# Two fused expert layers behind attention: the order of weight conversions, row loads and stores changed

## The chip, the core and the metric

One core of one Trainium2 chip runs the whole program. The metric is the time of one execution in microseconds (us). TensorE (PE) multiplies, VectorE (DVE), ScalarE (ACT) and GpSimd (POOL) do the rest, and DMAs move data between the chip's memory and the core. SyncE (SP) does no arithmetic: it issues DMAs, in the order of the program, and where one of them has to wait, all behind it on SP stand. GpSimd can issue DMAs too, on a queue of its own.

## The reference

```python
q_s = exp(q - max(q, -1)); q_s /= sum(q_s, -1) + 1e-09      # (8, 8, 576, 64)
k_s = exp(k - max(k, 2));  k_s /= sum(k_s, 2) + 1e-09
kv = einsum('bhsd,bhse->bhde', k_s, v)
x = einsum('bhsd,bhde->bhse', q_s, kv)                       # as rows: (4608, 512)
g = x @ w_gate                                               # 512 x 1536
x = (g * sigmoid(g) * (x @ w_val)) @ w_out                   # 1536 x 512
h = x @ w_in                                                 # 512 x 2048
y = where(h > 0, h, exp(min(h, 0)) - 1) @ w_out2             # 2048 x 512
```

All of it is float32.

## The kernel before

**Tiling.** The 4608 rows are nine blocks of 512. The first expert layer has d_ff 1536, twelve tiles f of 128; the second 2048, sixteen tiles. A float32 product is made of three products: each operand is split into a rounded part (hi, by ACT) and the rest (lo, by DVE).

**Phase A** (`run_a`, to about 570 us) takes the first six f of all nine blocks. A block i has 6 x 3 places (f, s): at s = 0 the gate projection, at s = 1 the value projection (`proj`, L828 to L832), at s = 2 the product with w_out of the f before (L809 to L811). The table `PLAN` puts the attention of block i+1 between them. At (2,1) and (2,2) the second half of the queries is normalized (L524 to L527, DVE) and turned, at (2,2) SP issues the loads of the turned queries (`in0`, tile qT, from dq), and at (4,0) they are multiplied with kv on PE (L639), into the PSUM banks "t" and "c".

The weights that later stages need arrive as raw blocks of 512 KB and are converted beside phase A, one stage of the pipe per call of `conv()`: SP loads a block (raw), ACT scales it (L199, tile cg), DVE makes its bits with three instructions (L214, L217 into PSUM bank "c", L221 out of it into the tile cd). There is one bank "c", so the queries' product into "c" waits until L221 has read it. In blocks 2 to 7 `conv()` is called at s = 2 of all six f and at (3,0): seven times. Rows of x of the block before are summed by GpSimd (L659, two per call of `store_x`) and stored to xs at (1,0) and (1,2).

Block 8 has `side_last` in place of the attention: it loads the rows of the first pair of blocks (`v_load`, eight DMAs of 256 KB), sums them on GpSimd (`v_sums`, eight subtractions L1389) and splits the results for the next phase (`x_make`, L1422 on ACT, L1423 on DVE).

**Phase B** (`run_b`, about 570 to 1000 us) does the other six f for pairs of blocks (0,1), (2,3), (4,5), (6,7), then for block 8 alone. A 2 x 2 block product takes seven products, M1 to M7 (L1118). A unit has six steps; the stationary rows s come two steps ahead into a ring of two, loaded by SP (`load_sb`, from sfg/sfv the first time, then from sbg/sbv). Between the steps the unit loads the next pair's rows (`v_load`), sums them (`v_sums`), and rebuilds the outputs of finished pairs for phase 2: SP loads yr from ys, GpSimd subtracts (L1019, tile xt), ACT and DVE split (L1063, L1035), GpSimd stores xd. The unit's end makes the split rows of the next pair. A block's rows are closed by DVE (L1474, tile ev) and stored to ys.

**Phase 2** (`run_2`, `step`) is the second layer in two halves over the same units, again with seven products per step, each summed by DVE (`add`, L1242) from PSUM into tiles u, the first copied there by ACT (L1264). The stationary rows of the next f are split inside a step: `split_pop()` does the ACT half (L1074), `lo_pop()` the DVE half (L1077). After half 0 of a unit its rows are stored to y2 (L1209).

The engines do their instructions in the order of this code; no scheduler reorders them.

Of the kernel before, what the change touches and what calls it, by code (L numbers as in the profile page):

```python
# [17 lines left out]
def kernel(  # L18
# [1068 lines left out]
    def split_pop():  # L1087
        if split_now:
            split_now.pop(0)()
            return True  # L1090
# [110 lines left out]
    def evac(half, blk, js):  # L1201
        if half == 0:
            ev = ev_p.tile([128, KD, TB], FP32, tag="ev", name="ev")
            for j in js:
                if j % 2:
                    nc.scalar.activation(out=ev[:, j, :], in_=acc["2", blk][j], func=ACTF.Copy)
                else:
                    nc.vector.tensor_copy(ev[:, j, :], acc["2", blk][j])
            nc.sync.dma_start(out=y2[blk], in_=ev)  # L1209
            return  # L1210
        ev = y2_t[blk]
        dst = out[blk * TB:(blk + 1) * TB, :]
        if blk >= TURN:
            dst = dst.rearrange("(j p) n -> p j n", j=4)
        else:
            dst = dst.rearrange("(p j) n -> p j n", j=4)
        for j in js:
            nc.vector.tensor_tensor(ev[:, j, :], acc["2", blk][j], ev[:, j, :], op=ALU.add)
            if len(js) == 1:
                nc.sync.dma_start(out=dst[:, j], in_=ev[:, j])  # L1220
        if len(js) > 1:
            nc.sync.dma_start(out=dst, in_=ev)
# [21 lines left out]
    def step(u, gs_, mid, after=None):  # L1244
        lo_pop()
        splits_due()
        d11, d12, d21, d22 = (dst_of(u, gs_, rc) for rc in ((0, 0), (0, 1), (1, 0), (1, 1)))
        prev = tail.pop() if tail else None
        p0 = p_bank(0)
        product(p0, "M1", u, gs_, True)  # L1250
        if prev:
            s0, b12, b21, e12, e21 = prev
            w = cg()
            add(w, s0, b12)
            add(s0, s0, b21)
        p1 = p_bank(1)
        product(p1, "M6", u, gs_, True)
        if prev:
            k21 = elu_act(s0, False)
        split_pop()  # L1260
        p3 = p_bank(3)
        product(p3, "M7", u, gs_, True)
        s1 = cg()
        nc.scalar.activation(out=s1, in_=p0, func=ACTF.Copy)  # L1264
        if prev:
            elu_stt(k21)
            elu_max(k21)
            k12 = elu_act(w, True)
        add(s1, s1, p1)
        if prev:  # L1270
            elu_hi(k21, e21)
        lo_pop()
        split_pop()
        split_pop()
        u3 = cg()
        add(u3, s1, p3)
        p2 = p_bank(2)
        product(p2, "M5", u, gs_, True)
        product(p0, "M2", u, gs_, False)
        add(u3, u3, p2)  # L1280
        if prev:
            elu_lo(k21, e21)
            elu_stt(k12)
            elu_max(k12)
        lo_pop()
        while split_pop():
            pass
        if after is None:
            k22 = elu_act(u3, False)
            if prev:  # L1290
                elu_hi(k12, e12)
            lo_pop()
            ends = [m() for m in mid]
            product(p2, "M3", u, gs_, False)
            product(p3, "M4", u, gs_, False)
            k11 = elu_act(p0, True)
            elu_stt(k22)
            elu_max(k22)
            if prev:
                elu_lo(k12, e12)  # L1300
            elu_hi(k22, d22)
            elu_stt(k11)
            elu_max(k11)
            elu_hi(k11, d11)
            elu_lo(k22, d22)
            elu_lo(k11, d11)
            for e in ends:
                if e:
                    e()
            tail.append((s1, p2, p3, d12, d21))  # L1310
            rot()
            return
        product(p2, "M3", u, gs_, False)
        product(p3, "M4", u, gs_, False)
        if prev:
            k11 = elu_act(p0, False)
            elu_hi(k12, e12)
            elu_lo(k12, e12)
        lo_pop()
        w = cg()  # L1320
        add(w, s1, p2)
        add(s1, s1, p3)
        for m in mid:
            m()
        if not prev:
            k11 = elu_act(p0, False)
        k21 = elu_act(s1, True)
        elu_stt(k11)
        elu_max(k11)
        elu_hi(k11, d11)  # L1330
        k22 = elu_act(u3, False)
        elu_stt(k21)
        elu_max(k21)
        elu_lo(k11, d11)
        elu_hi(k21, d21)
        elu_lo(k21, d21)
        elu_stt(k22)
        elu_max(k22)
        elu_hi(k22, d22)
        elu_lo(k22, d22)  # L1340

        def rest():
            k12 = elu_act(w, True)
            elu_stt(k12)
            elu_max(k12)
            elu_hi(k12, d12)
            elu_lo(k12, d12)

        rot()
        after(rest)  # L1350
# [17 lines left out]
    V = {}  # L1368
    V_SRC = {"M1": 0, "M7": 1, "M2": 2, "M3": 3, "M5": 4, "M6": 5, "M4": 6}

    def v_load(u):
        w = TB if len(u) == 2 else TB // 2
        V[u] = []
        for c in range(2):
            t, t_ = (
                w2_pool[0].tile([128, 4 - part, TB], FP32, tag=f"s{2 + c}{part}", name="v")
                for part in range(2)
# [93 lines left out]
    def b_evac(blk):  # L1471
        ev = yp_t.pop(blk)
        for c in range(KD):
            nc.vector.tensor_tensor(ev[:, c, :], acc["b", blk][c], ev[:, c, :], op=ALU.add)  # L1474
        nc.sync.dma_start(out=ys[blk], in_=ev)

    T, n_T = {}, [0]

# [192 lines left out]
    def unit_b(n, u, nxt, carry):  # L1671
        a, b = u
        for k, (kind, g) in enumerate(B_STEPS):
# [19 lines left out]
            ahead = B_STEPS[(k + 2) % len(B_STEPS)], n == 0 and k < len(B_STEPS) - 2  # L1693
            step_b(u, kind, g, mid, tick, ahead, last)
            load_sb(ahead[0], (1,), first=ahead[1])
            if k == 0:
                v_load(nxt)
            if k == 2:
                v_sums(nxt)
        b_D(a, F1 - 2)  # L1700
        ev = b_D(a, F1 - 1)
# [10 lines left out]
        if single:  # L1712
            x_make(nxt, head[2:])
            rest = ("M2", "M3", "M4")
        else:
            rest = ("M7", "M5", "M2")
        for op in rest:
            x_alloc(nxt, (op,))
            x_make(nxt, (op,))
# [5 lines left out]
    def single_b(u, carry):  # L1725
        NG1 = HALF // 2
        nxt = units[0]
        for g in range(NG1):
# [23 lines left out]
            if g == 0:  # L1752
# [2 lines left out]
                X[nxt] = ({}, [])  # L1755
                x_big(nxt, X_HEAD)
            if g == 1:
                load_s(0)
                load_s(1, 1)
                x_small(nxt, X_MID[2:], ANY)  # L1760
        while xd_st["k"] < 6 or later:
            aged()
            lo_pop()
# [21 lines left out]

    def side_last(ff, s):
        u = units[0]
        if (ff, s) == (0, 2):
            v_load(u)
        if (ff, s) == (1, 2):  # L1790
            v_sums(u)
            load_sb(B_STEPS[0], first=True)
            load_sb(B_STEPS[1], first=True)
        if (ff, s) == (2, 2):
# [2 lines left out]
            split_pop()  # L1797
        if (ff, s) == (2, 0):
            x_alloc(u, ("M1", "M6"))
            for op in ("M7", "M5", "M2"):  # L1800
                todo.append(lambda op=op: (x_alloc(u, (op,), ("w",)), x_make(u, (op,))))
            for f in range(HALF, F1):
                todo.append(lambda f=f: load_ob(f, ("w",)))
# [99 lines left out]
                st[name]()  # L1903

    pend_b = []

    def run_a():
        for i in range(NB):
# [5 lines left out]
            for f in range(HALF):  # L1914
                for s in range(3):
# [20 lines left out]
                    if i == 1 and (stage["split"] < NA1 or s == 2):  # L1936
                        conv()
                    side_1a(i, f, s)
                    if i and f == 1 and s != 1:
                        store_x(i - 1, s // 2)  # L1940
                    if s == 1:
                        silu_val(t, val, ("a", i, f))
                    elif s == 2:
                        split_lo()
                    if 2 <= i < NB - 1 and (s == 2 or (f, s) == (3, 0)):
                        conv()
                    if i == NB - 1:
                        if s:
# [122 lines left out]
```

## Time and profile before

| | before |
|---|---|
| runs | 1758.6, 1758.87, 1762.76 us; median 1758.87 |
| the profiled execution | 1761.39 us |
| its span | 1759.7 us |
| PE busy | 1682.6 us (96%), 8228 matmuls |
| DVE, ACT, POOL busy | 1200.3, 806.6, 309.6 us |
| mean granted TensorE clock | 0.984 |

The span runs from the first to the last instruction of the profiled execution, and 1.7 us lie around it. Waits are idle times of an engine, put down to what ended them. A row of the timeline is one instruction or a run of like ones: start, length, engine, line, operation, out<-in, shapes, and in brackets the idle time before it with what ended that. The granted clock of a window is its mean over that window; TensorE runs at 2.4 GHz (1.00) or at 1.2 GHz (0.5).

### The profile page before, as it was taken

The numbers are of one execution on the slowest core, as the hardware profiler recorded it, in microseconds if no ns is written. First come the engines' busy times: TensorE is split into PE (matmuls) and PEld (weight loads), VectorE is DVE, ScalarE is ACT, GpSimd is POOL, SyncE is SP. The second block draws the span as 40 slices with busy tenths as digits, with TensorE's granted clock in tenths as the row PEclk, the third lists the DMA queues.
The fourth block names the chain that finished last, engine by engine and source line by source line (L and its number), as shares of the span: only waits on it lengthen the run. The fifth ranks groups of instructions, "written<-read, shape, count | busy, mean of one in ns | idle before, by whom it ended". The sixth has DMA issues, their size and how long they took to land.

```text
span 1759.7 us, 22267 instructions
## 1 busy us (share of the span) xinstructions
PE 1682.6 (96%) x8228; PEld 1374.9 (78%) x8228; DVE 1200.3 (68%) x1808; ACT 806.6 (46%) x1347; POOL 309.6 (18%) x346
## 2 busy tenths in 40 slices
PE   5899989999998899999999989999999999999999
PEld 4677777777877688787888868888888988888887
DVE  7867898878756574665666686757674866556474
ACT  4644244334334332332424474646564655445362
POOL 3613342344215202232231000000000000000000
PEclk9999999999999999999999999999999999999999
DMA  9467977796574667577686927262623434251511
GB/s 284 115 159 204 280 216 213 232 288 214 191 248 176 227 242 243 216 286 303 249 321 224 390 67 269 96 248 77 250 84 126 165 153 164 99 196 68 215 48 72
DMA packets 183532, 348.29 MB, mean 198 GB/s; under 512 B 49920, under 2 KB 121856, under 8 KB 169984
## 3 DMA queue, kind: packets, MB, share of 16 engines
q1 hardware_dynamic: 167712, 285.79, 49.1%
q0 software_dynamic: 15712, 61.09, 9.0%
q8 instruction: 64, 1.05, 0.2%
q14 instruction: 44, 0.36, 0.1%
HBM read 230.69 MB, written 116.14 MB: 197 GB/s over the span
## 4 chain that ended last, share of the span: by engine, by line
PE 65%; DVE 16%; DMA 8%; ACT 4%; issue 3%; POOL 2%; SPq 1%; DVEq 0%; POOLq 0%; ACTq 0%
PE p L1118 26%; PE y L811 10%; PE y L809 10%; PE y L810 10%; PE a L828 3%; PE a L829 3%; PE a L832 3%; DMA s<-sd 2%; DVE u L1242 1%; DMA s<-sfv 1%; DVE g L847 1%; DVE c L217 1%; DMA s<-sbv 1%; POOL v L1389 1%; DVE c L214 1%
## 5 line engine op out<-in xcount | busy, mean ns | idle before, releaser
L1242 DVE TENSOR_TENSOR u<-u,p 128x512 f32<-128x512 f32 x315 | 216.0, 686 | 218.5 <-PE p L1118 200.0
L1118 PE MATMUL p<-xp,s 128*128 128x512 f32 x1344 | 323.2, 394 | 20.3 <-DVE u L1242 19.7
L1118 PEld LDWEIGHTS p<-xp,s 128*128 128x128 f32 x1344 | 253.5, 190 | 78.3 <-DVE u L1242 24.8
L1118 PE MATMUL p<-xs,s 128*128 128x512 f32 (+1 forms) x1260 | 272.6, 370 | 3.4 <-ACT u L1264 1.8
L1118 PEld LDWEIGHTS p<-xs,s 128*128 128x128 f32 x1260 | 222.5, 190 | 44.8 <-ACT u L1264 2.4
L811 PE MATMUL y<-w,g 128*128 128x512 f32 x576 | 225.1, 391 | 0.6
L810 PE MATMUL y<-w,g 128*128 128x512 f32 x576 | 224.3, 389 | 0.7 <-DVE w L1077 0.7
L809 PE MATMUL y<-w,g 128*128 128x512 f32 x576 | 224.2, 389 | 0.0
L828 PE MATMUL a<-x,w 128*128 128x512 f32 x424 | 173.3, 409 | 6.4 <-DVE th L859 5.1
L829 PE MATMUL a<-x,w 128*128 128x512 f32 x424 | 170.0, 401 | 0.0
L1137 DVE SCALAR_TENSOR_TENSOR th<-e,th 128x512 f32<-128x512 f32 x144 | 99.3, 690 | 101.0 <-ACT e L1132 99.6
L1130 ACT ACTIVATE e<-u 128x512 f32<-128x512 f32 x108 | 67.7, 627 | 150.9 <-DVE u L1242 150.9
L811 PEld LDWEIGHTS y<-w,g 128*128 128x128 f32 x576 | 108.1, 188 | 26.2 <-DVE g L1166 3.9
L810 PEld LDWEIGHTS y<-w,g 128*128 128x128 f32 x576 | 108.2, 188 | 23.3 <-DVE w L1077 1.1
L809 PEld LDWEIGHTS y<-w,g 128*128 128x128 f32 x576 | 108.1, 188 | 22.3
L1157 ACT ACTIVATE g<-th 128x512 fp32r<-128x512 f32 (+1 forms) x160 | 91.3, 580 | 67.9 <-DVE th L1143 67.9
L1166 DVE TENSOR_TENSOR g<-th,g 128x512 fp32r<-128x512 f32 (+1 forms) x160 | 100.0, 635 | 32.0 <-ACT g L1157 29.7
L832 PE MATMUL a<-x,w 128*128 128x512 f32 x424 | 115.0, 393 | 0.6 <-POOL w L254 0.6
L828 PEld LDWEIGHTS a<-x,w 128*128 128x128 f32 x424 | 82.4, 194 | 29.9 <-DVE th L859 5.5
L841 ACT ACTIVATE g<-th 128x512 fp32r<-128x512 f32 x54 | 34.0, 629 | 153.7 <-DVE th L859 153.7
L829 PEld LDWEIGHTS a<-x,w 128*128 128x128 f32 x424 | 82.8, 195 | 16.8
L832 PEld LDWEIGHTS a<-x,w 128*128 128x128 f32 x424 | 81.0, 191 | 18.4 <-POOL w L254 1.0
(222 smaller groups left out, 2803.0 us busy)
## 6 DMA issues: line engine op xcount, KB each, us to landing
xp<-xd SPq DMA_DIRECT2D x32, 1024.0 KB, 10.2
xs<-xd SPq DMA_DIRECT2D x51, 512.0 KB, 7.0
xd<-xst POOLq DMA_DIRECT2D x42, 512.0 KB, 9.0
raw<-in_moe_w_out SPq DMA_DIRECT2D x26, 512.0 KB, 5.6
s<-sbg SPq DMA_DIRECT2D x10, 1024.0 KB, 7.0
s<-sbv SPq DMA_DIRECT2D x10, 1024.0 KB, 6.9
yp<-ev SPq DMA_DIRECT2D x9, 1024.0 KB, 3.9
xs<-ev POOLq DMA_DIRECT2D x18, 512.0 KB, 4.1
```

The costliest lines, as they stand in the source:

```text
L809: nc.tensor.matmul(out=ps, lhsT=wh, rhs=xh, start=first, stop=False)
L810: nc.tensor.matmul(out=ps, lhsT=wh, rhs=xl, start=False, stop=False)
L811: nc.tensor.matmul(out=ps, lhsT=wl, rhs=xh, start=False, stop=last)
L828: nc.tensor.matmul(out=ps, lhsT=wh, rhs=x[:, c, 0, :], start=(c == 0), stop=False)
L829: nc.tensor.matmul(out=ps, lhsT=wh, rhs=x[:, c, 1, :], start=False, stop=False)
L832: nc.tensor.matmul(out=ps, lhsT=wl, rhs=x[:, c, 0, :], start=False, stop=(c == KD - 1))
L1118: nc.tensor.matmul(out=out_, lhsT=w, rhs=x, start=first and (q, c, k) == (0, 0, 0), stop=(c, k) == (1, 2), skip_group_check=True,)
L1130: nc.scalar.activation(out=e, in_=h, func=ACTF.Relu, scale=-1.0)
L1137: nc.vector.scalar_tensor_tensor(out=t, in0=e, scalar=1.0, in1=t, op0=ALU.add, op1=ALU.mult)
L1157: nc.scalar.activation(out=gt[:, 0, at:at + n], in_=t[:, q * n:(q + 1) * n], func=ACTF.Copy)
L1166: nc.vector.tensor_tensor(gt[:, 1, at:at + n], t[:, q * n:(q + 1) * n], gt[:, 0, at:at + n].bitcast(FP32), op=ALU.subtract,)
L1242: nc.vector.tensor_tensor(o, a, b, op=ALU.add)
```

## The change

In phase A the seven calls of `conv()` in blocks 2 to 7 stand in a table: the one at (3,2) is moved to (2,0). `store_x` is called at (2,1) and (3,0), in place of (1,0) and (1,2). In block 8 the two halves of `v_load` come at (0,0) and (0,1) in place of (0,2), and `v_sums` at (1,1) in place of (1,2). In phase B a half of `v_load` comes after step 1 and the other after step 2, in place of all of it after step 0, and `v_sums` after step 3 in place of step 2; the last rows of a pair are split in the order M2, M5, M7. The ys and y2 rows are stored by GpSimd's queue. In phase 2 one early `split_pop()` and one `lo_pop()` go, and the sum u3 comes ahead of the two splits that are left. In the unit of block 8 a split is put ahead of two loads.

```diff
-            nc.sync.dma_start(out=y2[blk], in_=ev)
+            nc.gpsimd.dma_start(out=y2[blk], in_=ev)
...
         product(p1, "M6", u, gs_, True)
         if prev:
             k21 = elu_act(s0, False)
-        split_pop()
         p3 = p_bank(3)
         product(p3, "M7", u, gs_, True)
         s1 = cg()
...
             elu_hi(k21, e21)
-        lo_pop()
+        u3 = cg()
+        add(u3, s1, p3)
         split_pop()
         split_pop()
-        u3 = cg()
-        add(u3, s1, p3)
         p2 = p_bank(2)
...
-    def v_load(u):
+    def v_load(u, cs=(0, 1)):
         w = TB if len(u) == 2 else TB // 2
-        V[u] = []
-        for c in range(2):
+        V.setdefault(u, [])
+        for c in cs:
...
-        nc.sync.dma_start(out=ys[blk], in_=ev)
+        nc.gpsimd.dma_start(out=ys[blk], in_=ev)
...
-            if k == 0:
-                v_load(nxt)
-            if k == 2:
+            if k in (1, 2):
+                v_load(nxt, (k - 1,))
+            if k == 3:
                 v_sums(nxt)
...
-            rest = ("M7", "M5", "M2")
+            rest = ("M2", "M5", "M7")
...
             if g == 1:
+                x_small(nxt, X_MID[2:], ANY)
                 load_s(0)
                 load_s(1, 1)
-                x_small(nxt, X_MID[2:], ANY)
...
-        if (ff, s) == (0, 2):
-            v_load(u)
+        if (ff, s) in ((0, 0), (0, 1)):
+            v_load(u, (s,))
+        if (ff, s) == (1, 1):
+            v_sums(u)
         if (ff, s) == (1, 2):
-            v_sums(u)
...
-            for op in ("M7", "M5", "M2"):
+            for op in ("M2", "M5", "M7"):
...
+    CONV_AT = ((0, 2), (1, 2), (2, 0), (2, 2), (3, 0), (4, 2), (5, 2))
...
-                    if i and f == 1 and s != 1:
-                        store_x(i - 1, s // 2)
+                    if i and (f, s) in ((2, 1), (3, 0)):
+                        store_x(i - 1, f - 2)
...
-                    if 2 <= i < NB - 1 and (s == 2 or (f, s) == (3, 0)):
+                    if 2 <= i < NB - 1 and (f, s) in CONV_AT:
                         conv()
```

On DVE, in a query block (here block 3), this is what the moved conversion passes: bd is the scaled kv, qr and q the queries' sums and the normalized queries, th and g the activation of the first layer and its lo half, km the keys' maximum, x the rows of the next block out of the banks "t" and "c".

```order
 L493 TENSOR_TENSOR bd_172<-t,rs 128x256
+L214 TENSOR_SCALAR c<-cg 128x512
+L217 SCALAR_TENSOR_TENSOR c<-cg,c 128x512
+L221 SCALAR_TENSOR_TENSOR cd<-raw,c 128x512
 L524 TENSOR_SCALAR qr<-qr 128x16
 L525 RECIPROCAL qr<-qr 128x16
```

```order
 L396 TENSOR_TENSOR km<-km,kr 64x512
 L847 TENSOR_TENSOR g<-th,g 128x512
-L214 TENSOR_SCALAR c<-cg 128x512
-L217 SCALAR_TENSOR_TENSOR c<-cg,c 128x512
-L221 SCALAR_TENSOR_TENSOR cd<-raw,c 128x512
 L648 TENSOR_TENSOR x<-t,x 128x512
 L648 TENSOR_TENSOR x<-c,x 128x512
```

The three instructions stood last ahead of the instructions L648 that read the queries' products, and stand now ahead of the second normalization, before the activation's product at (2,1).

SP in the first unit of phase B, before: s are stationary rows (sfg, sfv where they come from), v the next pair's rows out of xs, yp the partial outputs of block 8.

```order
L1440 DMA s_5055<-sfg_128 128x4x256
L1440 DMA s_5097<-sfg_129 128x3x256
L1386 DMA v<-xs_176 128x512
L1386 DMA v<-xs_177 128x512
L1386 DMA v<-xs_176 128x512
L1386 DMA v<-xs_177 128x512
L1386 DMA v<-xs_176 128x512
L1386 DMA v<-xs_177 128x512
L1386 DMA v<-xs_176 128x512
L1386 DMA v<-xs_177 128x512
L885 DMA yp_191<-ev 128x2048
L1440 DMA s_5162<-sfv_134 128x4x256
```

The same place now:

```order
L1438 DMA s_5055<-sfg_128 128x4x256
L1438 DMA s_5097<-sfg_129 128x3x256
L885 DMA yp_191<-ev 128x2048
L1438 DMA s_5150<-sfv_134 128x4x256
L1438 DMA s_5176<-sfv_135 128x3x256
L1384 DMA v<-xs_176 128x512
L1384 DMA v<-xs_177 128x512
L1384 DMA v<-xs_176 128x512
L1384 DMA v<-xs_177 128x512
L1438 DMA s_5235<-sfg_130 128x4x256
```

All eight loads of rows stood ahead of the stationary rows sfv; now sfv is first, and four loads of rows stand ahead of the next ones.

GpSimd in the third unit, before: xd are stores of rebuilt rows, yr and xt the subtractions that make them, v the sums of the next pair's rows.

```order
L1037 DMA xd_212<-xst 128x1024
L1389 TENSOR_TENSOR v<-v 128x512 x8
L1019 TENSOR_TENSOR xt<-yr 128x512
L1019 TENSOR_TENSOR xt<-yr,xt 128x512
L1019 TENSOR_TENSOR yr<-yr 128x512
L1037 DMA xd_217<-xst 128x1024
```

And now:

```order
L1019 TENSOR_TENSOR xt<-yr 128x512
L1019 TENSOR_TENSOR xt<-yr,xt 128x512
L1019 TENSOR_TENSOR yr<-yr 128x512
L1037 DMA xd_217<-xst 128x1024
L1019 TENSOR_TENSOR yr<-yr,xt 128x512
L1037 DMA xd_218<-xst 128x1024
L1037 DMA xd_220<-xst 128x1024
L1387 TENSOR_TENSOR v<-v 128x512 x8
L1037 DMA xd_221<-xst 128x1024
L1473 DMA ys_196<-ev 128x2048
```

The sums went behind the rebuilding of rows that stood behind them, and the store of ys stands behind them on GpSimd.

On PE the order of the instructions is the same in both.

## Rows read from the trace of the kernel before

**Rows 1.** Waits of PE: engine, line, what for: us in total, times, longest us.

```profile
PE p L1118 <- DVE u L1242: 22.6, 11, 5.6
...
PE t L639 <- DMA qT<-dq: 3.6, 2, 3.1
...
PE c L639 <- DVE cd L221: 10.2, 4, 4.3
...
PE a L828 <- DVE th L859: 5.1, 1, 5.1
```

**Rows 2.** Windows: stretch, length, busy PE PEld DVE ACT POOL, clock, DMA share, GB/s.

```profile
197.00:210.00 13.00, 10.19 (x48) 7.40 (x47) 10.56 (x19) 3.05 (x6) 5.75 (x11) 0.87 1.01 297
256.00:270.00 14.00, 9.16 (x39) 5.99 (x38) 10.81 (x20) 2.87 (x5) 6.84 (x9) 0.76 0.98 322
319.00:329.00 10.00, 7.30 (x34) 4.55 (x33) 6.91 (x12) 2.82 (x5) 4.23 (x7) 0.83 1.02 350
378.00:390.00 12.00, 8.90 (x38) 6.12 (x37) 5.62 (x10) 2.13 (x4) 4.90 (x8) 0.72 1.02 322
543.00:556.00 13.00, 7.92 (x23) 6.01 (x22) 10.84 (x12) 5.25 (x9) 8.52 (x11) 0.74 0.69 275
597.00:608.00 11.00, 5.36 (x18) 4.02 (x17) 5.12 (x7) 3.02 (x4) 4.16 (x5) 0.84 0.55 216
710.00:720.00 10.00, 5.83 (x19) 4.39 (x18) 7.88 (x11) 2.87 (x5) 3.26 (x5) 0.83 0.93 347
806.00:816.00 10.00, 8.03 (x28) 6.14 (x28) 8.09 (x13) 2.71 (x5) 2.67 (x4) 0.83 1.02 415
1012.00:1021.00 9.00, 5.81 (x20) 4.39 (x19) 6.75 (x12) 4.37 (x8) 0.00 (x0) 0.81 0.52 167
1355.00:1362.00 7.00, 4.12 (x32) 3.72 (x31) 4.65 (x8) 6.30 (x11) 0.00 (x0) 1.00 1.08 368
```

**Rows 3.** Timeline of DVE, POOL and PE in block 3: start, us, instruction.

```profile
238.68 3.35 DVE L847 TENSOR_TENSOR g<-th,g 128x512 fp32r<-128x512 f32 x1
...
238.96 2.51 POOL L659 TENSOR_TENSOR ev<-x 128x512 f32<-128x512 f32 x2
...
248.17 0.68 DVE L859 TENSOR_TENSOR th<-th,a 128x512 f32<-128x512 f32 x1
...
249.22 0.39 PE L828 MATMUL a<-x,w 128*128 128x512 f32 x1
...
250.65 0.67 DVE L847 TENSOR_TENSOR g<-th,g 128x512 fp32r<-128x512 f32 x1
...
262.25 0.69 DVE L221 SCALAR_TENSOR_TENSOR cd<-raw,c 128x512 uint32<-128x512 uint32 x1
...
262.99 0.68 PE L639 MATMUL c<-qT,bd 64*64 64x256 f32 x1 [4.34 <-DVE cd L221]
```

**Rows 4.** Timeline of ACT in block 8.

```profile
539.67 0.63 ACT L1422 ACTIVATE xp<-v 128x512 fp32r<-128x512 f32 x1 [6.00 <-POOL v L1389]
```

**Rows 5.** Timeline of SP in the first unit.

```profile
578.54 5.52 SPq L1386 DMA_DIRECT2D v<-xs  x8
```

**Rows 6.** Chain of waits in the first unit: start, us, what.

```profile
584.75 13.97 DMA s<-sfv
```

**Rows 7.** Timeline of POOL and ACT in the second unit.

```profile
695.23 11.61 POOL L1389 TENSOR_TENSOR v<-v 128x512 f32<-128x512 f32 x8
...
708.12 0.63 ACT L1063 ACTIVATE xst<-xt 128x512 fp32r<-128x512 f32 x1 [7.30 <-POOL xt L1019]
```

**Rows 8.** Timeline of ACT in phase 2, half 1's first unit.

```profile
1355.64 1.06 ACT L1074 ACTIVATE s<-s 128x1024 fp32r<-128x1024 f32 x1 [2.76 <-DMA s<-sd]
```

**Rows 9.** Waits of SP.

```profile
SPq L1008 <- DMA ys<-ev: 23.6, 3, 11.4
```

**Rows 10.** Page, part 6, DMA issues: out<-in, queue, count, KB, us to landing.

```profile
xd<-xst POOLq DMA_DIRECT2D x42, 512.0 KB, 9.0
...
yp<-ev SPq DMA_DIRECT2D x9, 1024.0 KB, 3.9
```

## Prediction

> **What bounds the kernel now.** The table of busy times says that PE is busy 1682.6 of 1759.7 us, and its instructions stand in the same order in both versions. So no edit can take work off PE; a gain is idle time of PE that goes, and a loss is idle time that comes. I read three views in this order: the waits of PE (what its idle times ended on), the windows around the longest of them (what each really cost), and the timelines of the engine that each waits for.
>
> The waits [rows 1] have four groups that the change touches: products L1118 behind a sum on DVE (22.6 us, 11 times), the queries' product into bank "c" behind the conversion's last instruction (10.2, 4 times), the queries' product behind the load of qT (3.6, twice), and the gate's projection in block 8 behind an activation product (5.1, once).
>
> An idle stretch costs more than its idle time. In the windows [rows 2] the cost is (length − PE busy) + (1 − clock) × length, the second part because at the lower of TensorE's two levels, 1.2 GHz, a stretch does half the work of 2.4. In block 3 (256 to 270): 14.00 − 9.16 = 4.84, and 0.24 × 14.00 = 3.36, together 8.2. The others by the same sum, in the rows' order: 4.5 (block 2), 8.2 (block 3), 4.4 (block 4), 6.5 (block 5), 8.5 (block 8), 7.4, 5.9 and 3.7 (units 0, 1, 2 of phase B), 4.9 (start of phase 2), 2.9 (its half 1's first unit; no fall of the clock after two short waits). That is 57 us in ten places. Nine contain a wait that an edit aims at; block 5 waits for qT, 3.10 us, which nothing here loads earlier.
>
> **A, conversions and sums in the query blocks.** The conversion moved is three DVE instructions of about 0.69 us [rows 3], 2.1 together. In block 3 its last one starts at 262.25 and PE's product into "c" at 262.99, after 4.34 idle. With it at (2,0), five places earlier, bank "c" is long free: a place is some 3.5 us (phase A's 570 us over 9 × 18 places). The wait occurs in blocks 2, 3, 4 and 6 (10.2 us in all; 0.34 in block 6). Removed at most: 4.5 + 8.2 + 4.4 + 0.3 = 17.4.
>
> What is late next: the qT loads. The qT waits are 3.6 in two [rows 1]: 3.1 in block 5 and so 0.5 in block 3. One raw block more of 512 KB is now asked for ahead of them on SP; at the 322 GB/s of these windows [rows 2], with the DMA share at about 1, that is 1.6 us. I charge 0.5 + 1.6 = 2.1 idle and 1.7 of clock (as in block 2's window) to block 3, and 1.6 each to blocks 4 and 5. A second price is on DVE: the three instructions now precede the activation's product L859 at (2,1), which ended at 248.85 while PE started the matmul that reuses its bank at 249.22 [rows 3]: 0.37 of slack against 2.1, so up to 1.8 per block, 10.8 for six. Against it stands the move of `store_x`: in block 3 L847 took 3.35 us beside GpSimd's two sums L659, and 0.67 alone [rows 3]. With the sums later, DVE reaches L859 2.7 us earlier, more than the 2.1 put in. I take these two as cancelling; the bounds are −3 and +10.8. The Trainium skill ("SBUF — State Buffer", section "Who interferes with whom") says that a DVE instruction with two SBUF inputs and a GpSimd instruction that reads SBUF exclude each other for a whole instruction; this trace agrees (3.35 against 0.67), and by that rule the sums, moved to (2,1) and (3,0), hold up another DVE instruction there instead, which would make the cancelling incomplete. A = −17.4 + 3.8 + 3.2 = −10.4, between −18 and +1.
>
> **B, block 8.** The idle time of 5.1 us [rows 1] hangs on the rows' sums: ACT waited 6.00 us for GpSimd's v until 539.67 [rows 4], and the splits that follow on DVE delay L859. The rows are now asked for one and two places earlier and summed one place earlier (3.5), and the two pairs of GpSimd sums L659, formerly ahead of them, come after (2 × 2.51 [rows 3]): 8.5 us sooner by this, over the 6.00. Cost now 8.5; I leave 1.5 for splits that then run beside the GpSimd sums. B = −7, between −8.5 and 0.
>
> **C, the units of phase B.** In unit 0 SP issued all eight v loads from 578.54, for 5.52 us [rows 5], 2 MB, and only then the stationary rows sfv, which took 13.97 us from 584.75 [rows 6]: the 5.64 us that PE stood idle in the window of unit 0 [rows 2] are the delay of their split. With sfv ahead, 2 MB less is in front of it; 2 MB at 216 to 350 GB/s are 6 to 10 us, over the wait. In unit 1 the v sums held GpSimd for 11.61 us from 695.23, and ACT's split of the rebuilt rows xt waited 7.30 behind them [rows 7]; the sums now come a step later. Unit 2 is alike. Half the v loads still stand ahead of each later stationary load, so a part stays: removed at most 7.4 + 5.9 + 3.7 = 17, and 0.5 of small waits; I leave 3. C = −14.5, between −17.5 and −3 (the wait moved by one step, with only unit 0 gained in half).
>
> **D, phase 2.** ACT's split of the stationary rows waited 2.76 for the load [rows 8], and the copy that frees s1 stood behind it on ACT; SP's load stood behind the y2 store, which waits for its evacuation. Now the copy comes first, and the store is on another queue: −2.9. At the start of phase 2 (4.9) u3 now comes ahead of two DVE splits: I take 2.0 of it; and 0.5 of other waits of the same form. D = −5.4, between −8 and +1 (splits that are now one place later can be late for the next product).
>
> **The sum.** −10.4 − 7 − 14.5 − 5.4 = −37.3. The profiled execution took 1761.4 us, 2.5 over the median of the runs: 1761.4 − 37.3 = 1724.1, and as a median 1721.6, so **1722**.
>
> **The rivals.** *Loads take over in the query blocks.* All of blocks 2 to 6 then wait for qT as block 5 does. For: the DMA share is 1.01, 0.98, 1.02 and 1.02 in the four windows [rows 2]. Against: in blocks 2 and 4 there was no wait for qT at all, though PE reached it only after "c". A falls to about −1 to −4: 1729 to 1738.
>
> *DVE takes over.* The inserted conversion makes L859 late in six blocks (+10.8), and in block 8, the units and phase 2 half of the 26.9 of B, C and D comes back as splits that are late (+13.5): 1722 + 24.3 = 1746, and 1733 with the first alone. For: 0.37 of slack. Against: the 2.7 that the sums no longer take.
>
> *Slower: stores on GpSimd land late.* Stores of 512 KB by GpSimd took 9.0 us to land where SP's of 1 MB took 3.9 [rows 10]: 5.1 more. ys rows are read back by SP, which stood 23.6 us in three waits for them already, the longest 11.4 [rows 9]; SP is in order, and the stationary rows stand behind. If each of the eight ys stores pushed a stall like block 8's (5.08 and 3.38 of clock [rows 2]) into PE, it would be 8 × 8.5 = 68: 1790. It decides once five of the eight do (42, 1764). Against: the code asks for a pair's rows only from the third step of the next unit on, and SP no longer stands at the evacuation itself. The Trainium skill ("DMA: Bandwidth & Descriptors", section "SWDGE vs HWDGE vs iDMA") sets plain transfers to the queues of SP and ACT, whose setup it calls faster, and leaves GpSimd those that cast or accumulate; the 9.0 against 3.9 agrees in sign. By that rule alone this edit loses, by the 5.1 per store where one is waited for.
>
> *No change:* the gains are given back by the raw loads and the later splits together, within 5.3 us of 1759.
>
> **How the numbers follow.** Forecast, 1708 to 1730: 0.58. Loads take over: 0.17. DVE takes over: 0.13. No change: 0.05. GpSimd's stores, or another net loss: 0.07. The forecast's own lower end is the sum of the full removals, 17.4 + 8.5 + 17.5 + 7 = 50, at 1709. The range holds the forecast, the first rival and most of the second, and a little of each side: 1704 to 1745. About 0.3% (5.3 us) is what a measurement can tell from no change; faster by more 0.88, within 0.05, slower 0.07.
>
> **What would show it.** In the waits of PE after the change: the group of "c" behind cd gone (A right), and the qT group at no more than 7 us (over 12: the first rival; L828 or L829 behind th in blocks 2 to 7: the second). The block 8 wait for th gone (B). In unit 0 the sfv load landing within 9 us of its issue, and ACT's wait for xt in unit 1 under 2 (C). In phase 2 the copy ahead of the split on ACT and no wait of PE for it (D). SP's waits for ys longer than 23.6 in all, with s loads behind them ending PE's waits, would show the slower rival. I am wrong in the mechanism if the waits go and the time stays: then others of the same length stand in the next row.

## The result

The changed kernel took 1735.86 us in the median of four runs (1733.9 to 1737.83), against 1758.73 before: ratio 0.9867, 95% interval 0.9847 to 0.9887. That is 22.9 us faster where 36.9 was forecast: the right sign, inside the range, and three fifths of the size. The profiled execution has a span of 1733.1 us against 1759.7. The time lies above the band of the forecast itself (1708 to 1730), in that of the first rival (1729 to 1738), but it is not that rival's doing: the waits for qT, which should then be over 12 us, are 4.6.

The waits of PE in the changed kernel, the answer to [rows 1] (engine, line, what for: us in total, times, longest):

```profile
PE p L1118 <- DVE u L1242: 13.0, 7, 4.1
...
PE y L810 <- DVE g L847: 5.9, 3, 3.2
PE t L639 <- DMA qT<-dq: 4.6, 3, 3.1
PE y L810 <- DVE w L1077: 4.2, 2, 2.3
...
PE a L828 <- DVE th L859: 2.4, 2, 1.9
```

The group of bank "c" (10.2) is gone and the wait for th is halved. But the sums u, 22.6 before, still cost 13.0, and two groups have grown: the lo half of w (0.7 before, 4.2 now) and g (3.2 before, 5.9 now). These are the places in which to look for the rest of the forecast.

PE's order is unchanged, so the same instruction can be looked up in both profiles. From the starts of a few of PE's instructions the difference builds up like this (us). "Block 1" and "block 7" are the second query products of these blocks, "phase B" its first product, "end of unit 0" the end of that unit's products, "block 8 alone" the first product of its unit, "phase 2" the last product ahead of it.

| from | to | before | after | difference | forecast |
|---|---|---|---|---|---|
| start | block 1 | 150.85 | 149.92 | −0.9 | 0 |
| block 1 | block 7 | 353.04 | 339.88 | −13.2 | −10.4 (A) |
| block 7 | phase B | 71.07 | 66.91 | −4.2 | −7 (B) |
| then | end of unit 0 | 66.32 | 60.69 | −5.6 | some −6 (C) |
| then | block 8 alone | 299.92 | 297.38 | −2.5 | the other −8 (C) |
| then | phase 2 | 52.71 | 51.96 | −0.8 | 0 |
| then | the last product | 761.12 | 761.54 | +0.4 | −5.4 (D) |

Together this is −26.8, where −37.3 was forecast for the profiled execution. It is more than the 22.9 of the medians mostly because the profiled execution of the kernel before took 1761.39 us, 2.7 over its median.

A was too small. B and C behind the first unit were too large, and of D nothing came.

What stands in C's place is seen in unit 2. The timeline of VectorE, GpSimd and PE there, in the changed kernel:

```profile
775.88 3.48 DVE L1496 TENSOR_TENSOR g<-th,g 128x512 fp32r<-128x512 f32 x2
...
777.52 12.34 POOL L1387 TENSOR_TENSOR v<-v 128x512 f32<-128x512 f32 x8
...
779.29 1.75 DVE L1035 TENSOR_TENSOR xst<-xt,xst 128x512 fp32r<-128x512 f32 x1
780.96 1.47 DVE L1242 TENSOR_TENSOR u<-u,p 128x512 f32<-128x512 f32 x2
...
781.69 2.75 PE L1118 MATMUL p<-xp,s 128*128 128x512 f32 x6 [3.41 <-DVE u L1242]
...
782.46 3.17 DVE L1488 TENSOR_TENSOR th<-th,u 128x512 f32<-128x512 f32 x2
```

GpSimd's eight sums of the next pair's rows now run for 12.34 us beside VectorE, and VectorE's instructions with both inputs in SBUF (not in PSUM, the banks that PE writes) take 1.5 to 1.8 us each here; the u that PE waits for stands behind three of them. L1242 itself, which reads one input from PSUM, is not stretched (1.47 for two).

The stores on GpSimd's queue are not slow. Part 6's view of the changed kernel and SP's waits for ys (the answer to [rows 9, 10]):

```profile
ys<-ev POOLq DMA_DIRECT2D x9, 1024.0 KB, 4.4
...
SPq L892 <- DMA ys<-ev: 53.8, 4, 14.3
...
SPq L1008 <- DMA ys<-ev: 11.8, 3, 5.8
```

From the same two views of the kernel before:

```profile
xs<-ev POOLq DMA_DIRECT2D x18, 512.0 KB, 4.1
...
SPq L1475 <- DVE ev L1474: 59.8, 8, 17.2
...
SPq L892 <- DMA ys<-ev: 18.3, 4, 6.1
```

The ys stores land in 4.4 us. But SP does not stand less for them. At L1008 it waits 11.8 us in place of 23.6, while at L892, where it loads yp into the tile ev that the store has to give back, it waits 53.8 in place of 18.3. Together these are 65.6 us in place of 41.9. What went is the 59.8 at L1475, where SP stood until the rows were closed.

### The profile page after: what moved, and what is told of

The parts are those of the page before. It is cut to its first block, busy times and chain, and to the rows that moved or that the text cites. A ratio compares the mean times of both kernels' runs of the same rounds, so it can differ in the third digit from the quotient of the medians.

```text
span 1733.1 us, 22290 instructions
## 1 busy us (share of the span) xinstructions
PE 1672.1 (96%) x8228; PEld 1367.2 (79%) x8228; DVE 1205.0 (70%) x1808; ACT 807.0 (47%) x1347; POOL 324.2 (19%) x364
## 4 chain that ended last, share of the span: by engine, by line
PE 70%; DVE 10%; DMA 6%; issue 5%; ACT 5%; POOL 2%; SPq 1%; DVEq 0%; POOLq 0%; ACTq 0%
PE p L1118 26%; PE y L811 11%; PE y L809 11%; PE y L810 11%; PE a L828 4%; PE a L829 4%; PE a L832 4%; DMA s<-sd 1%; DVE u L1242 1%; DMA ys<-ev 1%; DMA yr<-ys 1%; DMA xp<-xd 1%; PE t L639 1%; PE t L481 1%; ACT th L1131 1%
## 5 line engine op out<-in xcount | busy, mean ns | idle before, releaser
L1242 DVE TENSOR_TENSOR u<-u,p 128x512 f32<-128x512 f32 x315 | 215.9, 685 | 203.2 <-PE p L1118 188.5
L828 PE MATMUL a<-x,w 128*128 128x512 f32 x424 | 169.3, 399 | 4.2 <-DVE th L859 2.4
L829 PE MATMUL a<-x,w 128*128 128x512 f32 x424 | 166.5, 393 | 0.0
L809 PEld LDWEIGHTS y<-w,g 128*128 128x128 f32 x576 | 108.4, 188 | 23.6 <-ACT w L1074 0.8
L832 PE MATMUL a<-x,w 128*128 128x512 f32 x424 | 113.7, 390 | 0.0
L828 PEld LDWEIGHTS a<-x,w 128*128 128x128 f32 x424 | 80.4, 190 | 27.2 <-DVE th L859 3.7
L1131 ACT ACTIVATE th<-e 128x512 f32<-128x512 f32 x144 | 91.1, 633 | 4.6
L832 PEld LDWEIGHTS a<-x,w 128*128 128x128 f32 x424 | 80.0, 189 | 16.8
```

The costliest lines, as they stand in the source:

```text
L809: nc.tensor.matmul(out=ps, lhsT=wh, rhs=xh, start=first, stop=False)
L828: nc.tensor.matmul(out=ps, lhsT=wh, rhs=x[:, c, 0, :], start=(c == 0), stop=False)
L829: nc.tensor.matmul(out=ps, lhsT=wh, rhs=x[:, c, 1, :], start=False, stop=False)
L832: nc.tensor.matmul(out=ps, lhsT=wl, rhs=x[:, c, 0, :], start=False, stop=(c == KD - 1))
L1131: nc.scalar.activation(out=t, in_=e, func=ACTF.Tanh, scale=-0.5)
L1242: nc.vector.tensor_tensor(o, a, b, op=ALU.add)
```

## The experiments

Times are medians. Each run has runs of the kernel before that were taken beside it: 1758.52 us for e1, e2, e4 and e5, 1759.37 for e3, e6, e7 and e9, 1757.99 for e10 to e13.

**The query blocks: both parts, then each alone.** Three kernels made from the kernel before.

```diff
# e1_conv_rows: both; e7_conv_only: the first; e13_rows_only: the second
+    CONV_AT = ((0, 2), (1, 2), (2, 0), (2, 2), (3, 0), (4, 2), (5, 2))
-                    if 2 <= i < NB - 1 and (s == 2 or (f, s) == (3, 0)):
+                    if 2 <= i < NB - 1 and (f, s) in CONV_AT:
...
-                    if i and f == 1 and s != 1:
-                        store_x(i - 1, s // 2)
+                    if i and (f, s) in ((2, 1), (3, 0)):
+                        store_x(i - 1, f - 2)
```

> The kernel before with the first part alone: the conversion at (2,0) in place of (3,2), and the block's rows summed at (2,1) and (3,0). Lining up PE's instructions of the two profiles, the changed kernel gained 13.2 us over blocks 2 to 6, where my term A was 10.4. If the parts add up, this run is 13 us under before, 1746, with no wait of PE for bank c behind cd, and waits for qT of some 4 us in block 4. If it needed the other parts (the rival: the SP and GpSimd queues relieved by them), it gains 6 or less: 1753.

Both: 1739.68 us (1733.86 to 1747.13), ratio 0.989 (0.9854 to 0.9926), 18.8 under before. More than the 13 expected, because block 8 gained too. Its PE timeline:

```profile
529.23 0.50 PE L828 MATMUL a<-x,w 128*128 128x512 f32 x1 [1.89 <-DVE th L859]
...
583.68 1.65 PE L1118 MATMUL p<-xp,s 128*128 128x512 f32 x3 [4.86 <-DVE u L1242]
...
697.10 2.93 PE L1118 MATMUL p<-xp,s 128*128 128x512 f32 x6 [5.63 <-DVE u L1242]
```

Block 8's wait for th, 5.1 before, is 1.89, as in the changed kernel. Of the two edits that term B counts, only the later sums of rows are in this run, not the earlier loads and sums of the first pair. The long waits of the first two units are still there (4.86 and 5.63, where before had 5.64 and 4.17). No wait for "c" is left, and block 4 waits 3.35 for qT, as expected.

> The kernel before with the moved conversion alone, the block's rows summed and stored where they were. The two parts together took 18.8 us off, and in their profile PE's wait in block 8 was already 1.89 us in place of 5.08. If the conversion makes the gain of blocks 2 to 6 (13) and the later sums of rows that of block 8 (GpSimd stood 10.55 us at a row store's predecessor there), then here the waits for bank c are gone and block 8's 5.08 us is still there: about 1747. If the sums of rows at their old place no longer fit (my 1.8 us per block, at 0.37 of slack), waits of L828 for L859 of up to 1.8 us show in blocks 2 to 7: 1752. If the conversion's move alone is all of it: 1740.

The conversion alone: 1747.83, ratio 0.9933 (0.9907 to 0.9959), 11.5 under. Its PE timeline:

```profile
190.48 0.50 PE L828 MATMUL a<-x,w 128*128 128x512 f32 x1 [1.19 <-DVE th L859]
...
538.85 0.79 PE L828 MATMUL a<-x,w 128*128 128x512 f32 x1 [5.10 <-DVE th L859]
```

Here are the waits for L859 that I priced at up to 1.8 per block (1.19, 1.04, and 0.4 to 0.5 in two more), and in block 3 L847 still takes 3.35 beside L659. With the sums moved as well they are gone (the changed kernel has one of 0.53, at a later product): the two prices did cancel, as the prediction had them. Block 8's 5.10 is untouched.

> The kernel before with the later sums and stores of a block's rows alone, the conversion where it was. With the conversion alone 11.5 us went and block 8's wait stayed 5.10; with both 18.8 went and it was 1.89. If the sums of rows held up GpSimd and VectorE in block 8 by themselves, its wait is 1.89 here, L847 at (1,1) takes 0.67 us, bank c's waits are still there, and the time is 4 to 7 us under before: 1753. If the two parts only work together (the sums at (3,0) would meet the conversion at (3,2)): no gain, 1758.

The sums of rows alone: 1745.36, ratio 0.9927 (0.9909 to 0.9944), 12.6 under, about twice what the first theory gave; the second gave nothing. GpSimd's wait there, in the kernel before and in this one:

```profile
POOL ev L659 <- DMA yp<-ev: 111.4, 7, 21.4
```

```profile
POOL ev L659 <- DMA yp<-ev: 48.1, 5, 32.4
```

At its old place the sum needs a tile ev that the store of yp has not yet given back, and GpSimd stands for 111.4 us in blocks 2 to 8. The two totals are not alike: the 32.4 of the second is block 1's, whose 32.0 the profile of the kernel before puts down to another load. In blocks 2 to 8, 15.7 are left of the 111.4.

It is not this standing that delays bank "c". The timeline of VectorE in block 3, before:

```profile
256.25 1.11 DVE L391 TENSOR_TENSOR km<-km,k 128x512 f32<-128x512 f32 x1
...
259.62 1.20 DVE L847 TENSOR_TENSOR g<-th,g 128x512 fp32r<-128x512 f32 x1
```

And here, with PE:

```profile
235.54 0.70 DVE L847 TENSOR_TENSOR g<-th,g 128x512 fp32r<-128x512 f32 x1
...
250.48 0.69 DVE L391 TENSOR_TENSOR km<-km,k 128x512 f32<-128x512 f32 x1
...
253.01 0.68 DVE L847 TENSOR_TENSOR g<-th,g 128x512 fp32r<-128x512 f32 x1
...
255.12 0.69 DVE L221 SCALAR_TENSOR_TENSOR cd<-raw,c 128x512 uint32<-128x512 uint32 x1
...
255.86 0.43 PE L639 MATMUL c<-qT,bd 64*64 64x256 f32 x1 [0.88 <-DVE cd L221]
```

From the first of these L847 to L221 the timeline shows no pause of VectorE in either run. Before, that L847 took 3.35 us beside L659 [rows 3], and three later instructions (L391, L396, the next L847) took 1.11, 1.10 and 1.20 beside GpSimd's sums for the conversion (L262 to L265). Here they take 0.70 and 0.69, 0.68, 0.68. That is 4.0 us less ahead of L221, and block 3 waits 0.88 for "c" in place of 4.34. In block 2 the first L847 still meets L659 (2.81, from 3.39), and its wait for "c" falls only from 2.81 to 2.24.

In block 8 GpSimd's queue does count. Before:

```profile
530.17 12.54 POOL L1389 TENSOR_TENSOR v<-v 128x512 f32<-128x512 f32 x8
...
531.71 3.40 DVE L1423 TENSOR_TENSOR xp<-v,xp 128x512 fp32r<-128x512 f32 x2 [1.22 <-ACT xp L1422]
```

And here:

```profile
506.87 10.87 POOL L1389 TENSOR_TENSOR v<-v 128x512 f32<-128x512 f32 x8
...
525.58 1.29 DVE L1423 TENSOR_TENSOR xp<-v,xp 128x512 fp32r<-128x512 f32 x2 [5.41 <-ACT xp L1422]
...
534.92 0.50 PE L828 MATMUL a<-x,w 128*128 128x512 f32 x1 [1.85 <-DVE th L859]
```

The sums of the first pair stood behind the rows' sums and ran beside the splits L1423. Now they are over by then, the first pair of splits takes 1.29 in place of 3.40, and block 8's wait is 1.85.

So the two parts of A overlap (11.5 and 12.6 alone, 18.8 together). Both aim at the wait for "c": the conversion's move takes it away, the later sums take it from 10.2 to 4.3 us, and they mend block 8 too.

**The units: rows in halves alone.** The kernel before with the loads after steps 1 and 2 and the sums after step 3.

```diff
-            if k == 0:
-                v_load(nxt)
-            if k == 2:
+            if k in (1, 2):
+                v_load(nxt, (k - 1,))
+            if k == 3:
                 v_sums(nxt)
```

> The kernel before with the loads of the next pair's rows in halves after steps 1 and 2, and their sums after step 3, in phase B's units; all else as before. Theory of contention: the sums, some 11 us of GpSimd, now run beside VectorE's instructions with two inputs, which stretch (the changed kernel shows 3.31 us for two of L1496 and 1.77 for one of L1035, against some 0.67 each), so that the sum u comes late at the end of a step: the gain is the 8 us that the aligned profiles show for phase B, 1751, and PE's waits for u of 1 to 3.4 us in units 1 to 3 are here as well. By my term C it is 14.5: 1744, with those waits absent. If those waits come from the stores of ys on GpSimd, they are absent here and the gain is 14 too.

1751.68, ratio 0.9952 (0.9932 to 0.9972): 6.8 under, half of term C, and PE's waits of units 1 and 2 are those of the changed kernel (1.08 and 3.41) although ys is stored by SP:

```profile
707.39 1.65 PE L1118 MATMUL p<-xp,s 128*128 128x512 f32 x6 [1.07 <-DVE u L1242]
...
801.04 2.92 PE L1118 MATMUL p<-xp,s 128*128 128x512 f32 x6 [3.42 <-DVE u L1242]
```

The stores are not their cause.

**The units: what do the sums cost VectorE?** Three kernels made from the changed one.

```diff
# e5_sums_memset: the sums are not computed, the same tiles are filled
-                v_sums(nxt)
+                v_fill(nxt)          # nc.gpsimd.memset(o, 0.0) for t1, t2, m4, b12
# e6_sums_late
-            if k == 3:
+            if k == 4:
                 v_sums(nxt)
# e9_sums_dve: the same eight on VectorE, one per tick, what is left at the unit's end
-                v_sums(nxt)
+                todo.extend(v_parts(nxt))   # nc.vector.tensor_tensor(o, a, b, subtract)
```

> The changed kernel with the eight subtractions of the next pair's rows in phase B's units left out: GpSimd fills the same tiles with zeros at the same place, so the sums are not computed; block 8 keeps its own. Theory of contention: GpSimd now only writes, VectorE's L1496 and L1035 take their 0.67 us each there, PE's waits for u of 1.08, 3.41 and 1.70 us in units 1 to 3 and most of 1.40 in unit 0 go, with the low clock behind them: 8 to 10 us, 1727. Theory of late loads (the rows yr land 7.4 us after their issue, 5.5 before, and push VectorE's instructions together): the waits stay, 1733 to 1736.

1728.19 us (1725.75 to 1730.1), 7.7 under the changed kernel. Unit 2 again, VectorE, GpSimd and PE:

```profile
774.45 3.82 POOL L1389 MEMSET v<- 128x512 f32 x8
774.50 0.68 DVE L1035 TENSOR_TENSOR xst<-xt,xst 128x512 fp32r<-128x512 f32 x1
775.83 1.66 PE L1118 MATMUL p<-xp,s 128*128 128x512 f32 x6 [0.61 <-DVE u L1242]
...
776.60 1.29 DVE L1493 TENSOR_TENSOR th<-th,u 128x512 f32<-128x512 f32 x2
```

Beside fills L1035 takes 0.68 in place of 1.75, and the pair th<-th,u (the changed kernel's L1488) 1.29 in place of 3.17; PE waits 0.61 in place of 3.41. The waits of 1.40 and 1.08 in units 0 and 1 are gone too. Unit 3's did not go, against what was expected: 1.70 in the changed kernel, 1.98 here, 2.07 and 2.67 in the next two; no run takes it apart. A fill is also shorter (3.82 us for eight), so GpSimd's time alone could have done it. The next two tell.

> The changed kernel with the sums of the next pair's rows in the units done by VectorE, one per tick from step 4 on, in place of GpSimd; all values are computed. VectorE gets 8 instructions of 0.68 us per unit more, 5.4 us. Theory of contention: L1496 and L1035 take their 0.67 us again, which saves VectorE some 8 us per unit, and PE's waits for u in units 1 to 3 go as in the run that only filled: 1728 to 1731. If VectorE's share of work is the limit there, the waits stay or grow: 1736 or more.

1729.45 (1723.96 to 1733.29), ratio 0.9822 (0.9788 to 0.9857), all values computed:

```profile
772.62 0.68 DVE L1035 TENSOR_TENSOR xst<-xt,xst 128x512 fp32r<-128x512 f32 x1
773.95 1.66 PE L1118 MATMUL p<-xp,s 128*128 128x512 f32 x6 [0.67 <-DVE u L1242]
...
775.93 0.68 DVE L1387 TENSOR_TENSOR v<-v 128x512 f32<-128x512 f32 x1
```

The work that took GpSimd 12.34 us takes VectorE 8 × 0.68 = 5.4, and PE waits 0.67 in place of 3.41: VectorE loses less by doing the sums itself than by doing its own work beside them.

> The changed kernel with the sums of the next pair's rows one step later still (after step 4). Theory of contention with GpSimd: the waits for u at the end of steps 3 and 4 in units 1 to 3 (1.08, 3.41, 1.70 us) move to step 5 or to the unit's end, where VectorE's splits of the next rows wait for the sums: no gain unless VectorE has room there: 1733 to 1740. If only the meeting with the rebuilt rows (L1035) in steps 2 and 3 costs, they go: 1728.

1730.66 (1729.1 to 1732.02), ratio 0.9833 (0.9811 to 0.9856), 5.2 under the changed kernel. I had expected the waits to move to the unit's end; they mostly went, and one grew, in unit 3:

```profile
776.26 1.66 PE L1118 MATMUL p<-xp,s 128*128 128x512 f32 x6 [0.61 <-DVE u L1242]
...
870.59 2.66 PE L1118 MATMUL p<-xp,s 128*128 128x512 f32 x6 [2.67 <-DVE u L1242]
```

This fits a cost that lies in the meeting with the rebuilding of rows in steps 2 and 3, where VectorE has most to do; it does not show it by itself. The intervals of the ratio of this run and of the one with the sums on VectorE overlap that of the changed kernel (0.9847 to 0.9887); the run with fills, and the three further down that keep the sums on VectorE, are clear of it.

**The stores and phase 2's step, each undone in the changed kernel.**

```diff
# e3_stores_sp
-            nc.gpsimd.dma_start(out=y2[blk], in_=ev)
+            nc.sync.dma_start(out=y2[blk], in_=ev)
-        nc.gpsimd.dma_start(out=ys[blk], in_=ev)
+        nc.sync.dma_start(out=ys[blk], in_=ev)
# e4_step_old: the early split back, u3 behind the splits
+        split_pop()
         p3 = p_bank(3)
...
-        u3 = cg()
-        add(u3, s1, p3)
+        lo_pop()
         split_pop()
         split_pop()
+        u3 = cg()
+        add(u3, s1, p3)
```

> The changed kernel with the stores of ys and y2 on SP's queue again. In the changed kernel's trace the ys stores landed 4.4 us after their issue on GpSimd's queue, against 5.3 on SP's before. My slower rival says that GpSimd's stores cost: then this run is faster, up to 10 us. If SP's standing at the evacuations cost stationary loads: slower by 3 to 6 us, 1740, with the wait of 2.76 for s behind y2 at the second half's turn back on ACT. If only the turn needed it: 1 to 3 us slower.

1735.64 (1731.21 to 1737.73): the same as the changed kernel. Neither my slower rival nor the relief of SP shows in the time. SP waits 4.6 and 17.6 us for ys here (L1008 and L892), and 72.5 for the rows to be closed.

One wait of PE differs: in the unit of block 8 it waits 4.09 for a sum with the stores on GpSimd's queue, and 1.83 and 1.26 with them on SP's. GpSimd and VectorE there, in the changed kernel and in this one:

```profile
928.75 0.53 POOL L1473 DMA_DIRECT2D ys<-ev  x1 [7.22 <-DVE ev L1472]
...
929.90 1.60 POOL L1019 TENSOR_TENSOR xt<-yr 128x512 f32<-128x512 f32 x1
...
931.97 3.38 DVE L1077 TENSOR_TENSOR s<-s 128x768 fp32r<-128x768 f32 x1
```

```profile
927.48 1.31 POOL L1019 TENSOR_TENSOR yr<-yr 128x512 f32<-128x512 f32 x1
...
934.34 0.95 DVE L1077 TENSOR_TENSOR s<-s 128x768 fp32r<-128x768 f32 x1
```

On GpSimd the subtractions L1019 stand behind the store, which waits 7.22 us for the rows to be closed, and so they run beside the split L1077 that is ahead of the sum: it takes 3.38 us. With the stores on SP they are over before that split, and it takes 0.95.

> The changed kernel with phase 2's step as before (the early split back, u3 behind the splits). By my term D it is 5.4 us slower than the changed kernel: 1741. By the aligned profiles the new order nets nothing: PE's waits for the lo half of w, 2.29 and 1.91 us at the start of phase 2, would go, and waits for u of 3.2 us there and two of about 1.4 at the second half's turn would be back: 1736, within 3. If the early split alone cost the new waits and the turn was mended by the store's other queue, it is some 4 us faster: 1732.

1736.79 (1735.45 to 1738.76): the same too. PE at the start of phase 2, with the old step and in the changed kernel:

```profile
993.47 1.65 PE L1118 MATMUL p<-xp,s 128*128 128x512 f32 x6 [3.19 <-DVE u L1242]
```

```profile
999.21 0.50 PE L810 MATMUL y<-w,g 128*128 128x512 f32 x1 [2.29 <-DVE w L1077]
...
1353.36 1.70 PE L1118 MATMUL p<-xs,s 128*128 128x256 f32 x12 [0.81 <-ACT u L1263]
```

The waits for u became waits for w. At the turn to the second half either edit does by itself: with the old step no wait of PE over 0.3 is left there, with the stores on SP two, of 0.73 and 0.79.

**Three attempts at a faster kernel**, all on top of the sums on VectorE.

```diff
# e10_early_split: in step(), after M6
+        split_pop()
# e11_store8_late: in side_last
-        if (ff, s) == (3, 0):
+        if (ff, s) == (4, 0):
             store_x(NB - 1, 0)
-        if (ff, s) == (3, 2):
+        if (ff, s) == (4, 2):
             store_x(NB - 1, 1)
# e12_both: the two together
```

> The changed kernel with the sums of the next pair's rows on VectorE in the units (1729.5 by itself) and phase 2's early split put back, u3 still ahead of the two others. If the missing early split makes w late at the start of phase 2 (waits of L810 for w, 1.7 and 2.3 us, there in every run without it and under 0.7 in every run with it), these go, and u3 first keeps the wait for u at 3.2 us from coming back: 1726. If the split's VectorE half is what delays u, the waits change their name and the time stays: 1729 to 1730.

1726.47 (1725.48 to 1727.23), ratio 0.9821 (0.9806 to 0.9836). The time is that of the first theory, but the waits for w stay, so the early split by itself is not what they lack. What is left is that u3 stands ahead of the two others, and the `lo_pop()` that went with it; no run takes these two apart:

```profile
1007.83 0.68 PE L810 MATMUL y<-w,g 128*128 128x512 f32 x1 [2.70 <-DVE w L1077]
```

> The changed kernel with the sums of the next pair's rows on VectorE in the units, and block 8's own rows summed and stored at (4,0) and (4,2) in place of (3,0) and (3,2). In block 8 two splits of rows (L1421) took 3.48 us beside GpSimd's sums L659, 1.29 alone, and PE waited 1.9 for L859 behind them. Theory of contention: that wait goes, 2 to 4 us with the clock: 1727. If the splits are late by their count on VectorE, it stays: 1729 to 1730.

1724.97 (1723.07 to 1725.84), ratio 0.9814 (0.9798 to 0.9831). The wait for L859 in block 8 went, and a product next to it waits longer for g (0.36 in the run with the sums on VectorE alone):

```profile
528.89 0.50 PE L810 MATMUL y<-g,w 128*128 128x512 f32 x1 [2.75 <-DVE g L847]
```

> The two edits of the runs beside it together: the sum of what they bring, 1724 if both theories hold, 1729 if neither.

1726.48 (1723.65 to 1728.06), ratio 0.9819 (0.9805 to 0.9834): no better than either. Against each other the four kernels with the sums on VectorE (1725.0 to 1729.5) can't be told apart here. The interval of the fastest ends below that of the changed kernel, so it is faster than that one too.

## Why the prediction was right in sign and too large

**What bounds it** held: PE's order stayed, waits went, and the time followed. The slower rival fell: ys landed in 4.4 us from GpSimd's queue and 5.3 from SP's, and putting the stores back changed nothing in the time. One of its signs did come, since SP's waits for ys grew to 65.6 us; the prediction had read 23.6 for the kernel before, the group at L1008 alone, and left out the 18.3 at L892. Its price rested on the 9.0 us of xd, though the same page has xs, of the same size and on the same queue, at 4.1.

That the range holds the result is in part luck. Of the 10.5 us between −37.3 and −26.8, B lacks 2.8, C 6.4 and D 5.8, while A gave 2.8 more and places put at nothing gave 1.7. The rival in which VectorE takes over is near in its second part (13.5 us of B, C and D come back, by late instructions of VectorE; 15.0 are missing); its first part, a late L859 in six blocks, did not come.

**A** (−10.4) was under-estimated: −13.2 in blocks 2 to 7 (12.2 to 19.2 us less in the ten profiles with these query blocks, which differ there most in the wait for qT), and with block 8 and what follows the two edits alone give 18.8. The wait for "c" and the price on L859 came as told. Of what is late next, block 4 waits 3.15 and 1.03 for qT where I charged 1.6; block 5, which I left at 3.1 plus 1.6, waits 0.43. What I priced too narrowly is what the sums of rows do to VectorE: the 2.7 us stood only against the conversion's 2.1. But the stretched L847 stands ahead of L221 on the same engine, so that the later sums shorten the wait for "c" by themselves (4.34 to 0.88 in block 3, with the conversion at its old place).

**B** (−7) brought −4.2, and one of its two edits did it. It counted 3.5 us for the earlier loads and sums of the first pair and 5.0 for the sums of rows that stood ahead of them. The later sums of rows alone take block 8's wait from 5.1 to 1.85; with the earlier loads and sums as well it is 1.89. And 1.5 was left where 1.89 and a new wait of 1.95 for g stand (1.94 with the sums of rows alone).

**C** (−14.5) is the step that failed: "the sums now come a step later" counted the old wait as gone and gave VectorE nothing for what it would meet. It brought 6.8 alone, and −8.1 in the table's two rows: 1.08, 3.41 and 1.70 us of PE's idle time stand in units 1 to 3. The place of the sums was the matter and the early order of loads was right: unit 0's 5.64 fell to 1.40. I had the rule on contention in hand, and used it only for A. The Trainium skill ("SBUF — State Buffer", section "Who interferes with whom") says that a VectorE instruction with two SBUF inputs contends with a GpSimd instruction that reads SBUF, not with one that only writes. By that rule L1488 beside the sums stretches and beside the fills (L1493 in that run) does not: the trace has 3.17 and 1.29.

**D** (−5.4) failed at the two us for u3: PE now waits 2.29 and 1.91 for the DVE half of a split there. Lined up by PE's instructions, the changed kernel is 27.2 us ahead at the end of phase B, 24.8 before the turn and 26.8 at the end: what the turn gains (its waits of 2.9 went down to 0.81), the start of phase 2 had lost.

What stays open: why block 4's wait for qT differs between kernels that are the same up to there (1.6 to 5.4), what unit 3 waits for when the sums are off GpSimd, and which of phase 2's edits makes w late.

## What to carry to other kernels

Where an instruction is moved away from one that it delays, list what runs beside it at the new place, on the other engines too, and price that from a row of the same trace. Where an engine that is off the critical path stands, as GpSimd did for 111.4 us, ask what its work meets when it runs at last: in block 3 VectorE never waited for it, while the meeting cost VectorE 4.0 us. When two edits aim at the same wait, don't add them.

## What the runs showed of the hardware

Eight subtractions that take GpSimd 12.34 us take VectorE 5.4, and beside them VectorE's own instructions with two inputs in SBUF took some 2.5 times as long (3.17 against 1.29 for a pair); beside GpSimd's fills they did not stretch. Beside the sums L659 one took five times as long (3.35 against 0.67). The sum u, with one input in PSUM, did not stretch beside either (1.47 for two). Stores of 1 MB landed no later from GpSimd's queue (4.4 us) than from SP's (5.3). But what stood behind such a store on GpSimd ran later and met another instruction of VectorE (3.38 us in place of 0.95).

Idle times of 1.89 and 1.95 us in block 8 left the granted clock at 1.00 (2.4 GHz), while unit 2's window before has 0.83 with 1.97 idle [rows 2], so the length of one wait alone does not tell whether the clock falls; the prediction charged 1.7 us for it to a wait of 2.1 in block 3. The first of the two windows below is that one, the second that of unit 2 with its 3.41 (stretch, length, busy us of PE, PEld, DVE, ACT, POOL, clock, DMA share, GB/s; changed kernel):

```profile
524.00:540.00 16.00, 12.16 (x53) 9.36 (x52) 13.14 (x16) 8.07 (x14) 9.83 (x10) 1.00 0.70 269
...
776.00:784.00 8.00, 4.59 (x17) 3.37 (x16) 7.86 (x7) 0.46 (x2) 7.83 (x8) 0.87 1.03 413
```
